# Two-layer cluster attention kernel: the first batch's assignment scores computed as long rows, constants and load holds on another engine, loads in another order

## The chip, the core and the metric

The kernel runs on one core of a Trainium2 chip. The metric is the device time of one execution in microseconds. A core has TensorE (matmuls, results to PSUM), VectorE, ScalarE and GpSimd for elementwise work, and SyncE (SP), whose queue issues the DMAs here. The engines run side by side and wait for each other by semaphores; each works through its own instructions strictly in the order in which the program has them.

## What is computed

Inputs are q, k, v of shape (2, 8, 768, 64): batch, heads, tokens, head size; 16 centroids per head; and four weight matrices. Everything is float32. Each query and each key goes to the centroid with the highest cosine, and a query attends only to keys of its own cluster. Then two MLPs follow.

```python
q_assign = argmax(einsum('bhsd,hcd->bhsc', q_n, c_n), axis=-1)   # same for k
mask = q_assign[:, :, :, None] == k_assign[:, :, None, :]
scores = where(mask, scale * q @ k.T, -1e9)
attn = softmax(scores)                # over keys
x = (attn @ v) -> (1536, 512)
h = x @ w_in;  g = h * clip(h + 3, 0, 6) / 6;  x = g @ w_out      # 512 -> 2048 -> 512
h = x @ w_in2; g = softplus(h);                out = g @ w_out2
```

## The kernel before

**Blocks.** Tokens are worked in six blocks of 256 queries (`b`, `u`: two batches, three blocks each), and in each block eight heads `h` with two chunks `c` of 128 queries: 96 chunks in all. A chunk (`chunk`) is: score matmuls into `s` (L811), the row maximum `nm` on VectorE (L814), the exponential `e` with its sum `sm` on ScalarE (L822), the constants `r0` (L824) and its reciprocal `r` (L826) on VectorE. Block 0 then works in float32: GpSimd makes a diagonal matrix `dg` of `r` (L835), TensorE transposes and scales `e` with it (`tr`, L842), ScalarE or VectorE copies to `pt`, and `avt` multiplies with v (L912). Later blocks split `e` times `r` into two float16 halves `hl` (ScalarE L433, VectorE L441) and transpose by DMA (L850).

**Assignment.** Before a pair of heads `p` can be scored, `assign(b, p)` finds the clusters. For the first batch it takes each 128 tokens of q or k as the stationary operand and streams the 16 centroids of one head past them (L714): 24 float32 matmuls, each of which is two records in the trace. The scores stand token by row in `asc`. VectorE takes the maximum of each 16 (`mx`, L718) and marks it (`eq`, L720); `et` (L725, twelve matmuls into quarters of 32 rows) turns the marks into rows, ScalarE copies them (`eb`, L727), `z` (L729) with the constant matrix `firstb` drops double marks, and VectorE writes the one-hot rows `oh` (L731). `rows` sends these by DMA under q and k (L758 for the first pair, L760 through DRAM for the others), where they carry the mask into the score matmuls. Block 0 has q and k zero-padded from 64 to 128 rows (`load0`).

**Weights.** They come as raw 64-bit words and are decoded on VectorE (`st<-raw`, L499 to L501), scaled by a power of two from a sum over all elements (`ams`, L418) and split into two float16 halves `w`. A raw tile can be written as soon as its buffer is free; to hold its load back, `pace` writes one column of it from the latest `r` on VectorE (L411), and `after` one from an `oh` on GpSimd (L404). The load waits for that write.

**Order.** The program's text, sorted by a table of due times (`plan`, from the numbers `K`), gives the first order. `own_order` then schedules all instructions with estimated durations (`list_schedule`) and fixes each engine's order and each buffer's turn by it. The chip only sees the fixed orders.

Of the kernel before, what the change touches and what calls it, by code (L numbers as in the profile page):

```python
# [24 lines left out]
    'slack': (184, 150),  # L25
    'a0': [-1.034, 0.017, 0.1, 0.301],
    'v0': 0.083,
    'v1': 3.174,
    'a1': [2.227, 2.112, 2.976, 3.115],
    'i': [0.443, 0.618, 0.93, 1.054],  # L30
    'il': [0.3, 0.468, 0.282, 0.282],
    'o': [1.198, 1.398, 1.598, 1.883],
    'ol': [0.192, 0.221, 0.231, 0.162],
    'wd': 0.075,
    'm': [1.41, 2.61, 3.54, 4.619, 5.555],
    'ml': [0.976, 0.75, 1.091, 1.101, 1.097],
# [21 lines left out]
    'w2e': [4.608, 4.84],  # L58
    'w2l': 0.64,
    'w2d': 0.213,  # L60
    't3': 4.134,
    'w2s': 'left',
    'te': [0, 0, 1, 0, 0, 0, 0, 0, 1, 0, 0, 0, 0, 0, 0, 0],
    'dgb': 2,
    'v2': -0.023,
# [5 lines left out]
    'vp': [-0.109, -0.075, -0.065, -0.073],  # L71
    'eqp': [0, 1, 1, 1],
# [30 lines left out]
def estimate(op, eng, ins, outs, inst, psum):  # L103
# [55 lines left out]
def graph(nc):  # L159
# [10 lines left out]
    T, stream = [], []  # L170
# [69 lines left out]
    g.insts, g.E, g.T, g.stream, g.tiles, g.after, g.needs = insts, E, T, stream, tiles, after, needs  # L240
# [4 lines left out]
def list_schedule(g, slack):  # L245
# [49 lines left out]
    for _ in range(N):  # L295
        best = None
        for e, r in ready.items():
            shared = port["Pool" if e == "DVE" else "DVE"] if e in port else 0.0
            for k in r:
                s = max(free[e], at[k])  # L300
                if T[k][2]:
                    s = max(s, shared)
                if best and (s, k) >= best:
                    continue
# [4 lines left out]
                if not best or (s, k) < best:  # L309
                    best = s, k  # L310
# [4 lines left out]
        if e == "PE":  # L315
# [3 lines left out]
            if cold:  # L319
                hold += stream[k]  # L320
# [50 lines left out]
def kernel(ctx: ExitStack, tc: tile.TileContext, qT, kT, v, cen, w1i, w1o, w2i, w2o, out):  # L371
# [208 lines left out]
    cur = {}  # L580
# [47 lines left out]
    cs0 = acon.tile([64, NP, 2, C], F32)  # L628

    def centroids():  # L630
# [70 lines left out]
    def assign(b, p):  # L701
        NT = S // 128
        a = cur["as"].tile([128, 2, NT, 2, C], F32, tag="h", name="asc")
        if b:
            rq, rk = load_q(b, p, slice(0, S), rawq), load_k(b, p)
        for t in range(2):
            for i in range(NT):
                c = slice(i * 128, (i + 1) * 128)
                if b:
                    nc.tensor.matmul(out=a[:, t, i], lhsT=(rq, rk)[t][:, c], rhs=cs[:, p], start=True, stop=True)  # L710
                    continue
# [532 lines left out]
```

## Time and profile before

| | us |
|---|---|
| median of 3 runs | 804.05 |
| lowest to highest | 801.77 to 806.32 |
| the profiled execution | 803.36 |
| its span, first to last instruction | 801.4 |
| TensorE busy | 754.5 (94%) |
| VectorE busy | 496.7 (62%) |
| ScalarE busy | 465.2 (58%) |
| GpSimd busy | 93.0 (12%) |

Busy shares are means over the whole span. The kernel has parts with different limits, so a stretch has to be read by itself. The chain of waits goes back from the last instruction to what released it, and so on to the start: what stands in it was on the path to the end, in that execution.

### The profile page before, as it was taken

How to read it: one execution, taken by the hardware profiler on the slowest of the kernel's cores; microseconds unless marked ns; L12 is line 12 of the kernel's file. 1: busy time of each engine (PE TensorE's matmuls, PEld its weight loads, DVE VectorE, ACT ScalarE, POOL GpSimd, SP SyncE). 2: the span in 40 equal slices, each digit the busy share in tenths (PEclk: the TensorE clock that was granted, in tenths of full speed). 3: DMA queues.
4: the chain of work that ended last, by engine and by line, in shares of the span. 5: the costliest groups of instructions: out<-in, count | busy, mean ns of one | idle time of the engine just before them, and what ended most of it. 6: DMA issues, size and time to landing. Idle time of an engine off the chain costs nothing.

```text
span 801.4 us, 13944 instructions
## 1 busy us (share of the span) xinstructions
PE 754.5 (94%) x5341; PEld 531.1 (66%) x5341; DVE 496.7 (62%) x1016; ACT 465.2 (58%) x797; POOL 93.0 (12%) x77
## 2 busy tenths in 40 slices
PE   5899986789899999989899999999999999999998
PEld 5677664568778888778787888965654444444443
DVE  3256899999987779877889996598342012100200
ACT  1064887777787879856887782668675134321400
POOL 6001720220110120000001000212402000000000
PEclk9998997889999999999999999999999999999999
DMA  8280659788987997889998989145010000000000
GB/s 178 52 281 21 203 186 224 189 189 208 230 219 165 186 193 152 158 176 221 219 183 169 226 198 280 55 141 175 13 40 14 14 13 14 14 13 14 14 27 26
DMA packets 182785, 106.06 MB, mean 132 GB/s; under 512 B 143808, under 2 KB 169280, under 8 KB 182720
## 3 DMA queue, kind: packets, MB, share of 16 engines
q1 hardware_dynamic: 182720, 105.19, 55.6%
q8 instruction: 42, 0.69, 0.4%
q14 instruction: 23, 0.19, 0.1%
HBM read 57.77 MB, written 7.86 MB: 82 GB/s over the span
## 4 chain that ended last, share of the span: by engine, by line
PE 68%; DVE 19%; DMA 7%; issue 3%; ACT 2%; SPq 1%; ACTq 0%; DVEq 0%
PE y L557 9%; PE y L558 9%; PE y L556 9%; PE h L556 8%; PE h L558 8%; PE h L557 8%; PE s L811 6%; PE asc L714 4%; PE avt L916 3%; DVE nm L814 3%; DVE hl L441 3%; DMA pt<-hl 2%; DMA raw<-in_moe_w_in_dram 2%; DVE st L500 2%; DVE w L441 2%
## 5 line engine op out<-in xcount | busy, mean ns | idle before, releaser
L556 PE MATMUL y<-g,w 128*128 128x256 f16 (+1 forms) x576 | 177.6, 309 | 1.3 <-ACT ys L997 1.3
L557 PE MATMUL y<-g,w 128*128 128x256 f16 (+1 forms) x576 | 177.6, 308 | 0.9 <-DVE g L441 0.9
L558 PE MATMUL y<-g,w 128*128 128x256 f16 (+1 forms) x576 | 177.5, 308 | 0.0
L556 PEld LDWEIGHTS <-w 128*128 128x128 f16 x1152 | 114.9, 100 | 62.7 <-issue 8.4
L557 PEld LDWEIGHTS <-w 128*128 128x128 f16 x1152 | 113.7, 99 | 63.1 <-issue 9.2
L558 PEld LDWEIGHTS <-w 128*128 128x128 f16 x1152 | 113.6, 99 | 60.4 <-issue 5.7
L441 DVE SCALAR_TENSOR_TENSOR g<-a,sg,g 128x512 f16<-128x512 f32 x48 | 37.1, 804 | 143.7 <-ACT g L433 143.6
L556 PE MATMUL h<-x,w 128*128 128x256 f16 x384 | 107.1, 279 | 3.2 <-DVE r L980 2.2
L557 PE MATMUL h<-x,w 128*128 128x256 f16 x384 | 106.7, 278 | 0.0
L558 PE MATMUL h<-x,w 128*128 128x256 f16 x384 | 106.7, 278 | 0.0
L822 ACT ACTIVATE e<-s,nm 128x768 f32<-128x768 f32 x96 | 85.7, 893 | 25.2 <-DVE nm L818 8.9
L814 DVE TENSOR_REDUCE nm<-s 128x1 f32<-128x768 f32 x96 | 90.8, 948 | 15.3 <-PE s L811 15.0
L441 DVE SCALAR_TENSOR_TENSOR hl<-e,r,hl 128x768 f16<-128x768 f32 x80 | 80.5, 1011 | 11.7 <-ACT hl L433 11.4
L433 ACT ACTIVATE hl<-e,r 128x768 f16<-128x768 f32 x80 | 73.6, 927 | 15.4 <-DMA pt<-hl 11.0
L557 PE MATMUL h<-y,w 128*128 128x512 f16 x192 | 72.8, 379 | 0.0
L558 PE MATMUL h<-y,w 128*128 128x512 f16 x192 | 72.8, 379 | 0.0
L556 PE MATMUL h<-y,w 128*128 128x512 f16 x192 | 72.6, 379 | 0.0
L1143 ACT ACTIVATE a<-h,c 128x512 f32<-128x512 f32 x48 | 31.9, 682 | 68.7 <-PE h L558 68.7
L916 PE MATMUL avt<-pt,v 128*64 128x256 f16 x720 | 52.3, 288 | 3.8 <-DMA pt<-hl 3.2
L811 PE MATMUL s<-kb,qb 128*128 128x384 f32 x160 | 49.8, 391 | 4.7 <-ACT e L822 3.1
L1181 ACT ACTIVATE os<-y,c 128x512 f32<-128x512 f32 (+1 forms) x13 | 8.4, 654 | 76.8 <-PE y L558 76.8
L787 POOL TENSOR_TENSOR kb<-rk,kb 64x768 fp32r<-64x768 f32 x16 | 31.7, 1984 | 153.0 <-ACT kb L786 152.6
(154 smaller groups left out, 1104.0 us busy)
## 6 DMA issues: line engine op xcount, KB each, us to landing
raw<-in_moe_w_out_dram SPq DMA_DIRECT2D x32, 512.0 KB, 4.8
raw<-in_moe_w_in_dram SPq DMA_DIRECT2D x8, 1024.0 KB, 7.6
raw<-in_moe_w_in_dram SPq DMA_DIRECT2D x16, 512.0 KB, 4.7
ka<-kb SPq DMA_DIRECT2D x40, 192.0 KB, 3.3
qd<-in_q_dram SPq DMA_DIRECT2D x80, 64.0 KB, 3.2
rk<-in_k_dram SPq DMA_DIRECT2D x12, 384.0 KB, 3.9
st<-in_v_dram SPq DMA_DIRECT2D x12, 256.0 KB, 4.1
ydram<-ys SPq DMA_DIRECT2D x12, 256.0 KB, 2.7
```

Source lines behind the costliest of these rows:

```text
L433: nc.scalar.activation(out=hi, in_=src, func=ACTF.Copy, scale=scale)
L441: nc.vector.scalar_tensor_tensor(out=lo, in0=src, scalar=scale, in1=hi, op0=ALU.mult, op1=ALU.subtract)
L556: nc.tensor.matmul(out=ps, lhsT=wt.lhsT(kk, m, 0), rhs=xh, start=start, stop=False)
L557: nc.tensor.matmul(out=ps, lhsT=wt.lhsT(kk, m, 0), rhs=xl, start=False, stop=False)
L558: nc.tensor.matmul(out=ps, lhsT=wt.lhsT(kk, m, 1), rhs=xh, start=False, stop=stop)
L714: nc.tensor.matmul(out=a[:, t, i, odd], lhsT=x[:, c], rhs=cs0[:, p, odd], start=True, stop=True)
L787: nc.gpsimd.tensor_tensor(out=kb[there], in0=rk[here], in1=kb[here].bitcast(F32), op=ALU.subtract)
L811: nc.tensor.matmul(out=s[:, n, 0:SH], lhsT=x[:, q], rhs=y[:, n * SH:(n + 1) * SH], start=i == 0, stop=i == len(pairs) - 1)
L814: nc.vector.tensor_reduce(out=nm, in_=sv, op=ALU.max, axis=AX.XY, negate=True)
L822: nc.scalar.activation(out=e.rearrange("p (a s) -> p a s", a=2), in_=sv, func=ACTF.Exp, bias=nm, scale=scale, accum_out=sm)
L916: nc.tensor.matmul(out=a[64 * odd:64 * odd + 64, p % 2, :], lhsT=vt[:, kt, vi, odd, :], rhs=PT[2 * p + odd][:, pi * KT + kt, :], start=(kt ...
L1143: nc.scalar.activation(out=a, in_=h, func=ACTF.Softplus, scale=cj)
```

## The change

- **Scores as long rows** (`assign`, first batch only). The centroids are now the stationary operand, 32 columns (one head's 16 and 16 zeros), and 384 tokens of q or k stream past them; eight matmuls, two for each quarter of 32 rows of one PSUM tile `asc`. ScalarE copies it to `sa`; three transposes on TensorE give `at`, token by row, for `mx` and `eq`. `et` is now three matmuls of 128 columns. `cs0` gets 128 rows and zeros. For pairs 0 to 2, `at` and `z` lie in another PSUM pool.
- **Constants.** `r0` is computed on GpSimd in blocks 2, 3 and 4 (48 chunks).
- **Holds.** `pace` uses GpSimd's `after` instead of a VectorE copy.
- **Order.** The planner has a limit on how far the DMA queue may run ahead (`back`), expects DMA results 800 ns late instead of 184, prices float32 matmuls otherwise, and the table `K` has new numbers.
- `right` and the pairs in `G` are assertions at build time; they make no instruction.

```diff
 K = {
-    'slack': (184, 150),
+    'slack': (800, 150),
+    'asx': 3,
+    'back': 10000,
+    'pcp': 1,
+    'r0p': [2, 3, 4],
...
@@ list_schedule
+            floor = queue - K["back"] if e == "SP" else 0.0
...
-                s = max(free[e], at[k])
+                s = max(free[e], at[k], floor)
...
@@ pace
         if 0 in paced:
-            nc.vector.tensor_copy(out=tile_[:, 0:1].bitcast(F32), in_=paced[0])
+            if K["pcp"]:
+                after(tile_, paced[0])
+            else:
+                nc.vector.tensor_copy(out=tile_[:, 0:1].bitcast(F32), in_=paced[0])
@@ centroids
-    cs0 = acon.tile([64, NP, 2, C], F32)
+    cs0 = acon.tile([128, NP, 2, 2, C], F32)
...
-        nc.vector.tensor_copy(out=cs0, in_=ctv[0:64])
+        for half in range(2):
+            nc.vector.tensor_copy(out=cs0[0:64, :, half, half, :], in_=ctv[0:64, :, half, :])
@@ assign, first batch
-                for odd in range(2):
-                    x = (Q0[p][0:64, odd], K0[2 * p + odd][0:64])[t]
-                    nc.tensor.matmul(out=a[:, t, i, odd], lhsT=x[:, c], rhs=cs0[:, p, odd], start=True, stop=True)
+            ac = cur["as"].tile([128, SH], F32, tag="h", name="asc")
+            for r in range(4):
+                t, n = divmod(r, 2)
                 for odd in range(2):
+                    x = (Q0[p][:, odd], K0[2 * p + odd])[t][:, n * SH:(n + 1) * SH]
+                    nc.tensor.matmul(out=ac[32 * r:32 * r + 32, :], lhsT=cs0[:, p, odd].rearrange("p a c -> p (a c)"), rhs=x, start=odd == 0, stop=odd == 1)
+            sa = asp.tile([128, SH], F32, tag="sa", name="sa")
+            nc.scalar.activation(out=sa, in_=ac, func=ACTF.Copy)
+            pool, tag = (ps_a, "a") if p < K["asx"] else (cur["as"], "h")
+            a = pool.tile([128, H2, 128], F32, tag=tag, name="at")
+            for i in range(H2):
+                nc.tensor.transpose(out=a[:, i, :], in_=sa[:, i * 128:(i + 1) * 128], identity=ident)
...
+            for i in range(H2):
+                nc.tensor.matmul(out=et[:, i * 128:(i + 1) * 128], lhsT=eq[:, i * 128:(i + 1) * 128], rhs=identb, start=True, stop=True)
@@ chunk
-        nc.vector.tensor_scalar(out=r0, in0=sm, scalar1=1e-9, scalar2=P14, op0=ALU.add, op1=ALU.mult)
+        (nc.gpsimd if (b * NU + u) in K["r0p"] else nc.vector).tensor_scalar(out=r0, in0=sm, scalar1=1e-9, scalar2=P14, op0=ALU.add, op1=ALU.mult)
```

Two places show how the order moves. TensorE, from the end of the first assignment on, before (L714 is an assignment's scores; q_184 and k_187 are the first pair's q and k, q_193 and k_196 the second's):

```order
L729 LDWEIGHTS firstb
L729 MATMUL z<-eb,firstb 128x384
L714 MATMUL asc<-cs_156,q_193 128x16 x12
L714 MATMUL asc<-cs_156,k_196 128x16
L714 MATMUL asc<-cs_156,k_199 128x16
```

And changed, from the second pair's first scores to the first score matmuls of attention (L735 is the new form; q_195, k_198 and k_201 are the second pair's, q_186 and k_189 the first's):

```order
L735 MATMUL asc<-q_195,cs_156 32x384
L760 LDWEIGHTS firstb
L760 MATMUL z<-eb,firstb 128x384
L735 MATMUL asc<-q_195,cs_156 32x384 x3
L735 MATMUL asc<-k_198,cs_156 32x384
L735 MATMUL asc<-k_201,cs_156 32x384
L735 MATMUL asc<-k_198,cs_156 32x384
L735 MATMUL asc<-k_201,cs_156 32x384
L741 MATMUL at<-ident,sa 128x128 x3
L849 MATMUL s<-k_189,q_186 128x384 x2
```

The second pair's scores now begin ahead of the first pair's `z`, and the second pair's transposes stand ahead of the first `s`. On VectorE the operations that build `firstb` stood behind the first `eq`; now all but the last two stand ahead of the first `mx`.

GpSimd, in blocks 0 and 1, before (L404 is a hold on `oh`, L835 `dg`, L787 the `kb` subtraction of the next block's keys):

```order
L404 TENSOR_SCALAR rk<-oh 128x1 x2
L835 TENSOR_SCALAR dg<-ident,r 128x128 x2
L787 TENSOR_TENSOR kb<-rk,kb 64x768
L835 TENSOR_SCALAR dg<-ident,r 128x128
L787 TENSOR_TENSOR kb<-rk,kb 64x768 x2
```

And changed (L416 is a hold, on `oh` or on `r`; L874 `dg`, L818 `kb`):

```order
L416 TENSOR_SCALAR rk<-oh 128x1 x2
L874 TENSOR_SCALAR dg<-ident,r 128x128 x2
L416 TENSOR_SCALAR raw<-r 128x1
L818 TENSOR_TENSOR kb<-rk,kb 64x768
L874 TENSOR_SCALAR dg<-ident,r 128x128
L818 TENSOR_TENSOR kb<-rk,kb 64x768
L874 TENSOR_SCALAR dg<-ident,r 128x128
L416 TENSOR_SCALAR raw<-r 128x1
L416 TENSOR_SCALAR qd<-r 128x1
L416 TENSOR_SCALAR raw<-r 128x1
L874 TENSOR_SCALAR dg<-ident,r 128x128
```

The holds of `raw`, `qd` and `rk` now stand between `dg` and `kb`. On VectorE, 32 `raw` copies, two of `rk` and one of `qd` are gone, and so are 48 of the 96 `r0`. Between VectorE's 17th and 33rd `nm`, where 12 `w<-st,wf` of L441 stood, 8 stand now, and the other four behind; one `hl`, one `mx` and four decode operations have also gone behind it, and two `qb` have come in.

## Rows read from the trace of the kernel before

**Rows 1.** Stretches: us; busy of PE, PEld, DVE, ACT, POOL; clock; DMA share; GB/s.
```profile
33.80:112.20 78.40, 74.81 (x444) 53.91 (x441) 55.19 (x129) 47.00 (x87) 24.75 (x27) 0.93 0.54 169
112.20:205.60 93.40, 74.41 (x564) 59.17 (x563) 92.93 (x196) 73.81 (x131) 10.49 (x6) 0.87 0.87 200
205.60:472.70 267.10, 258.53 (x2344) 216.09 (x2344) 228.50 (x457) 207.14 (x376) 21.02 (x12) 0.98 0.91 190
```

**Rows 2.** Two `nm` reductions in the timeline: start us, us, engine, line.
```profile
112.16 0.94 DVE L814 TENSOR_REDUCE nm<-s 128x1 f32<-128x768 f32 x1
...
205.56 0.93 DVE L814 TENSOR_REDUCE nm<-s 128x1 f32<-128x768 f32 x1
```

**Rows 3.** The chain that ended last, in order of time: start us, us, what.
```profile
6.64 10.43 PE asc L714 x48
...
33.85 1.58 PE s L811 x2
...
35.75 3.84 PE s L811 x6
...
51.92 6.15 PE asc L714 x48
...
58.07 2.86 PE tr L842 x12
...
60.93 2.54 PE s L811 x4
...
65.48 1.45 PE avt L912 x12
...
66.93 1.53 PE tr L842 x12
...
68.47 5.67 PE asc L714 x48
...
77.00 1.34 PE s L811 x4
```

**Rows 4.** Stretches of 2 us: TensorE busy us, granted clock, DMA share, GB/s.
```profile
6.00:8.00 2.00, 1.63 (x8) 1.00 1.01 212
...
36.00:38.00 2.00, 2.00 (x4) 1.00 0.31 96
...
58.00:60.00 2.00, 2.00 (x10) 0.50 0.04 16
```

**Rows 5.** The first assignment's steps in the timeline.
```profile
17.10 0.56 DVE L718 TENSOR_REDUCE mx<-asc 128x24 f32<-128x384 f32 x1 [10.14 <-PE asc L714]
...
18.92 0.49 ACT L727 ACTIVATE eb<-et 128x384 bf16<-128x384 f32 x1 [15.66 <-PE et L725]
...
20.39 0.50 PE L729 MATMUL z<-eb,firstb 128*128 128x384 bf16 x1 [1.55 <-DVE firstb L624]
...
20.92 0.68 DVE L731 TENSOR_SCALAR oh<-z,lim 128x384 f32<-128x384 f32 x1 [0.60 <-PE z L729]
...
22.95 1.22 SPq L758 DMA_DIRECT2D q<-oh  x2
```

**Rows 6.** The landing of its rows (DMA issues: KB each, us to landing).
```profile
q<-oh SPq DMA_DIRECT2D x4, 24.0 KB, 2.4
```

**Rows 7.** TensorE in the timeline where two tile shapes follow each other.
```profile
63.40 0.37 PE L725 MATMUL et<-identb,eq 128*32 128x128 bf16 x12
63.71 1.51 PE L912 MATMUL avt<-pt,st 128*64 128x256 f32 x10
```

**Rows 8.** VectorE from 112 to 206 us, groups: busy us, mean ns, idle before.
```profile
L441 DVE SCALAR_TENSOR_TENSOR w<-st,wf,w 128x512 f16<-128x512 f32 x12 | 10.0, 868 | 0.0
...
L411 DVE COPY raw<-r 128x1 f32<-128x1 f32 x15 | 1.8, 142 | 0.0
```

**Rows 9.** GpSimd's `dg`: the group of 16, then one in the timeline.
```profile
L835 POOL TENSOR_SCALAR dg<-ident,r 128x128 f32<-128x128 f32 x16 | 15.6, 977 | 43.2 <-DVE r L826 16.0 <-PE tr L842 7.0 <-DVE st L499 6.5
...
68.62 1.96 POOL L835 TENSOR_SCALAR dg<-ident,r 128x128 f32<-128x128 f32 x1 [6.52 <-DVE st L499]
```

More of the change, by code (lines that the diff above doesn't have):

```diff
@@ L57 @@
     'ze': [0],
[L58 to L61, printed above, removed]
+    'w2e': [4.647, 4.705],
+    'w2l': 0.276,
+    'w2d': 0.437,
+    't3': 4.102,
     'w2s': 'left',
[L63 removed]
+    'te': [1, 0, 1, 0, 0, 0, 0, 0, 1, 0, 1, 0, 0, 0, 0, 0],
     'dgb': 2,
[L65 removed]
+    'v2': -0.269,
     'dge': 0,
@@ L169, in graph @@
     wrote, read, bank = {}, {}, {}
-    T, stream = [], []
+    T, stream, cold = [], [], []
     def cells(a):
@@ L192, in graph @@
         stream.append(elements(ins[0]) * min(i.tile_size[1], 128) / 76.8 if E[k] == "PE" and str(ins[0].dtype) == "dt.float32" else elements(ins[0]) / 2.4 if E[k] == "PE" else 0.0)
+        cold.append(max(stream[k], 1.75 * i.tile_size[1]) if E[k] == "PE" and str(ins[0].dtype) == "dt.float32" else stream[k])
         T.append(estimate(i.opcode, E[k], ins, outs, i, psum))
@@ L239, in graph @@
     g = Graph()
-    g.insts, g.E, g.T, g.stream, g.tiles, g.after, g.needs = insts, E, T, stream, tiles, after, needs
+    g.insts, g.E, g.T, g.stream, g.cold, g.tiles, g.after, g.needs = insts, E, T, stream, cold, tiles, after, needs
     g.users, g.group, g.order, g.bufs, g.pool = users, group, order, bufs, pool
@@ L308, in list_schedule @@
                 s = max(s, w)
-                if not best or (s, k) < best:
-                    best = s, k
+                least = min(least, s)
+                own.append((k, s))
+            own = [(s, k) for k, s in sorted(own) if s <= least + look][:1]
+            if own and (best is None or own[0] < best):
+                best = own[0]
         s, k = best
@@ L319, in list_schedule @@
             if cold:
-                hold += stream[k]
+                hold += g.cold[k]
                 done = hold + 170
@@ L721, in assign @@
         et = cur["as"].tile([128, SH], F32, tag="h", name="et")
-        for t in range(2):
-            for i in range(NT):
-                r0, c0 = 32 * (2 * t + i * 128 // SH), i * 128 % SH
-                nc.tensor.matmul(out=et[r0:r0 + 32, c0:c0 + 128], lhsT=eq[:, (t * NT + i) * 32:(t * NT + i + 1) * 32], rhs=identb, start=True, stop=True)
+        if b:
+            for t in range(2):
+                for i in range(NT):
+                    r0, c0 = 32 * (2 * t + i // H2), i % H2 * 128
+                    nc.tensor.matmul(out=et[r0:r0 + 32, c0:c0 + 128], lhsT=eq[:, (i * 2 + t) * 32:(i * 2 + t + 1) * 32], rhs=identb, start=True, stop=True)
+        else:
+            for i in range(H2):
+                nc.tensor.matmul(out=et[:, i * 128:(i + 1) * 128], lhsT=eq[:, i * 128:(i + 1) * 128], rhs=identb, start=True, stop=True)
         eb = asp.tile([128, SH], BF16, tag="eb", name="eb")
         nc.scalar.activation(out=eb, in_=et, func=ACTF.Copy)
-        z = cur["as"].tile([128, SH], F32, tag="h", name="z")
+        pool, tag = (ps_a, "a") if b == 0 and p < K["asx"] else (cur["as"], "h")
+        z = pool.tile([128, SH], F32, tag=tag, name="z")
         nc.tensor.matmul(out=z, lhsT=firstb, rhs=eb, start=True, stop=True)
@@ L798, in prep, with right @@
         KQ[h] = (qa, qb, ka, kb)
+        of["q", h] = b, u
         rows(b, u, h)
     PT = {}
+    of = {}
+    def right(which, b, u, h):
+        if of.get((which, h), (0, 0)) != (b, u):
+            raise ValueError("another block's tile")
     def chunk(b, u, h, c):
         p, odd = divmod(h, 2)
+        right("q", b, u, h)
         qa, qb, ka, kb = KQ[h] if b + u else (Q0[p][:, odd], None, K0[h], None)
@@ L990, in l2 @@
             for kk in range(4 * part, 4 * part + 4):
-                g = G[kk // 2]
+                of, g = G[kk // 2]
+                if of != i:
+                    raise ValueError("a later block's g")
                 mm3(y[:, m % 2, :], W1O, kk, m, g[:, 0, kk % 2, :], g[:, 1, kk % 2, :], kk == 0, kk == KF - 1)
```

66 lines of the change are left out of this document (36 added, 30 removed).

## Prediction

> **What bounds the kernel now.** I read the busy time of long stretches first, then the chain of waits, then single rows where the chain passes the code that changes. In the stretches [rows 1] one engine after another is full. From 33.8 to 112.2 us TensorE is busy 74.8 of 78.4 us. From 112.2 to 205.6, VectorE is busy 92.9 of 93.4 us and TensorE only 74.4. From 205.6 on TensorE is nearly full again (258.5 of 267.1 us), and so it stays to the end. The borders are no accident: at 112.16 and 205.56 the 17th and the 33rd of the 96 `nm` reductions start [rows 2], one for each chunk, so the first stretch is block 0's sixteen chunks and the second is block 1's. Before 33.8 us there are only the first two assignments.
>
> The chain of waits [rows 3] shows what the first stretches consist of. The assignment's `asc` matmuls hold 10.43 us of it from 6.64, the same again from 21.66 for the second pair of heads, 6.15 us from 51.92 and 5.67 us from 68.47: 32.7 us, all on TensorE and all on the path. The first score matmul, `s`, starts only at 33.85. Two things are to be seen in the single times. First, an `asc` record costs the same however little it streams: 16 columns, but 10.43/48 = 0.22 us. Second, TensorE runs at two speeds. `s` takes 3.84/6 = 0.64 us at 35.75 and 1.34/4 = 0.335 us at 77.00; twelve `tr` take 2.86 us at 58.07 and 1.53 us at 66.93. The granted clock [rows 4] prints 0.50, that is 1.2 GHz, in 58 to 60 (and so again in 74 to 76), each time just after one of the two later `asc` runs; around 36 us it prints 1.00, but the 0.64 us of `s` says that TensorE was at the lower level there too, as it was under the first two `asc` runs (0.22 us a record, against 5.67/48 = 0.12 at 68.47).
>
> **The change part by part.** *Scores as long rows.* Of the first batch's four assignments each had 24 float32 matmuls (48 records), which go. In come 8 matmuls of 384 columns into 32 output rows (16 records), a ScalarE copy `sa`, and three transposes (6 records). No row of before shows a float32 matmul into 32 columns. The nearest is the first block's `avt`, 64 columns wide, with neighbours that alternate between the two halves of the array: 12 records of 256 columns in 1.45 us [rows 3], 0.121 us each; scaled to 384 columns 0.181. Lower bound: all four quarters run at once, four records deep, by `s` 4 x 0.335 = 1.34 us at full clock and 2.56 us at the lower one. Upper bound: none overlap, 16 x 0.335 = 5.4 us or 10.2 us. I take the `avt` price, since two neighbours in a row go to one quarter here: 2.9 us at full clock, 5.8 us at the lower one. The transposes are priced by `tr`: 6/12 of 1.53 = 0.77 us, or of 2.86 = 1.43 us.
>
> *Start.* Assignment 0 begins at 6.64 as before, since the same centroid chain releases it. Scores to 12.4; `sa`, priced as the copy `eb`, 0.49 us and a hand-over of 0.1 [rows 5], to 13.0; transposes to 14.4. From `mx` (17.10) to the end of `oh` (20.92 + 0.68 = 21.60) the trace has 4.50 us [rows 5], in which `z` at 20.39 waited 1.55 us for `firstb`. The order now builds `firstb`'s parts ahead of `mx`, so `z` can start 0.1 us behind `eb` (18.92 + 0.49), at 19.5, not 20.4: 0.9 us less; two short VectorE operations get in between, by the price of a hold 0.2 us each with their gaps [rows 8]. So 4.0 us, and `oh` ends at 18.4 instead of 21.6. Its rows then go out by four DMA issues, of which the last begins 0.6 us before 24.17 and lands 2.4 us later [rows 5, 6]: 4.4 us after `oh`, 22.8. Meanwhile TensorE does the second assignment: one matmul ahead of `z`, seven behind it (14 x 0.36 at the lower clock = 5.1 us, to about 22.6), `sa` 0.6, transposes 1.4. The order puts the first `s` behind these, so it starts at 24.6 instead of 33.85: **9.2 us**. With the lower bound it is 13: the scores end at 10.5, since k's second half is the sixth load (1.6 MB at 212 GB/s [rows 4] from 2.4 us on lands at 10), `oh` at 16.4, and the rows land at 20.8. With the upper bound it is 0.7: scores to 16.9, `z` at 22, then 14 x 0.64 and 2 us more, so `s` at 33.1.
>
> *Assignments 2 and 3* lie inside the stretch where TensorE is full. They had 6.15 + 5.67 = 11.8 us and will have 2 x (2.9 + 0.77) = 7.3: **4.5 us** (bounds 7.6 and -0.5). *Clock:* what ran at 1.2 GHz behind those two `asc` runs was twelve `tr` (2.86 against 1.53) and `s` (2.54 against 1.34) at 58.07 to 63.5, and a second such `tr` run at 74: 1.3 + 1.2 + 1.3 = **3.8 us**. The new records stream 384 columns as `s` does, and behind runs of `s` and `avt` the clock doesn't fall in these stretches; I take all of it, with 0 as the other end.
>
> A rule speaks against this part. The trace has 12 `et` of 32 columns at 63.40 and `avt`, with another shape, at 63.71 [rows 7]: no idle stands between them. The Trainium skill (TensorEngine Tiling, Key Properties) says that changing the tiling mode drains TensorE; the trace gives no visible price for it. The same section says that different tiles run in parallel, which is the lower bound above, and one of the rivals.
>
> *Constants and holds to GpSimd.* Between the 17th and the 33rd `nm`, VectorE now has 15 `raw` holds at 0.142 us [rows 8], which go (2.1 us). The order also moves work out of this stretch to behind it: four `w<-st,wf` at 0.868 us [rows 8] (3.5 us), and one `hl`, one `mx` and four decode operations, while two `qb` move in; I put these six at half of that row each, 2.6 us. VectorE is full there, so up to 8.2 us. But DMA is at 0.87 of its time in that stretch [rows 1]; in 85 us it would be at 0.96. I take half, 4.1, and take back 2 us, since the order also leaves TensorE that much more to do behind the 33rd chunk: **2.1 us**. Constants `r0` of blocks 2 to 4 (48 operations) leave VectorE where it is busy 228.5 of 267.1 us while TensorE is full [rows 1]: nothing, and what hides it is TensorE. If that cover went, each would cost what a `dg` takes more than a hold, 0.84 us [rows 8, 9].
>
> *Loads.* The order of SP's queue moves v's loads behind the first weight loads, and little else. The queue's bounded backlog changes what the planner believes; with DMA at 0.54 in the first stretch I cost it at nothing, with 4 us either way for the 8.6 us that TensorE still waits in 205.6 to 472.7 [rows 1].
>
> Sum: 9.2 + 4.5 + 3.8 + 2.1 = 19.6 us. The profiled execution took 803.36 us for its span of 801.4, so 783.8 us; the median of the runs is 0.7 us above it. I say **784 us**.
>
> **The rivals.** *Four quarters at once*: 13 + 7.6 + 3.8, and with it the whole 8.2 us of VectorE's stretch, 32.6: 771 us. For it: the 12 `et` of 32 columns issue within 0.31 us [rows 7], 26 ns each. Against it: two matmuls in a row go to one quarter. (This is the Trainium skill's rule on tiles, named above.)
>
> *No overlap*: the new form doesn't shorten what it replaces: 0.7 - 0.5 + 3.8 + 2.1 = 6.1, so 797 us. Against it: `avt` at 0.121 us, where one stream of 256 columns by the `s` row would be 0.22.
>
> *GpSimd's holds in the way.* A hold stands in front of a load, in GpSimd's strict order, between `dg` and `kb`; the SP queue and VectorE's decode wait behind it. GpSimd operations next to VectorE's are slow at times: `dg`, 128 columns, takes 0.977 us on average and 1.96 us at 68.62 [rows 9]. If each of the 15 holds delays its load by that mean, all of it on the path, 15 x (0.98 - 0.14) = 12.6 us of the gain is lost: 796 us. At 1.96 us each it is 27.3 us, and the kernel is **slower, 811 us**. The point from which it is slower is 19.6/15 + 0.14 = 1.4 us a hold. Against it: GpSimd is busy 10.5 of 93.4 us in that stretch [rows 1], and a load sent a microsecond late mostly lands in time. For it, the Trainium skill (GPSIMD Engine Reference, Specifications) says that GpSimd shares its SBUF interfaces with VectorE; the two times of `dg` don't speak against it, and no row here shows the cause.
>
> **How the numbers follow.** Forecast 784 (777 to 791 on its own): 0.50. Four quarters, 771: 0.20. No overlap, 797: 0.13. Holds at 1 us, 796: 0.10. Holds at 2 us, 811: 0.07. A measurement of this kernel tells about 0.5% from no change, 4 us. Faster by more than that: 0.5 + 0.2 and most of the two at 796 and 797, 0.88. Within it 0.06, slower 0.06. The range leaves out the slow case and the far end of the quick one: 769 to 798 us, which holds about 0.85.
>
> **What would show it.** The first `s` at 24 to 25 us (21 under four quarters, 33 without overlap), 16 `asc` records in about 5.8 us at the start and 2.9 us later; a granted clock that doesn't fall to 0.50 behind assignments 2 and 3; the 17th `nm` at about 95 us instead of 112.2, and the 33rd at about 184 instead of 205.6; from there to the end 595 to 600 us as now (801.4 - 205.6 = 596). The forecast is wrong if the gain at the 17th `nm` is gone at the 33rd, or if TensorE idles more than 9 us between the 33rd and the 96th. Holds in the way would show as SP's loads waiting for GpSimd, and VectorE idle before a decode.

## The result, and the profile after

The changed kernel takes **784.7 us** (median of 4 runs, 782.4 to 786.5) beside 804.1 us for the kernel before: a ratio of 0.976, 95% interval 0.972 to 0.980. The forecast was 784.0 us in a range of 769 to 798. The profiled execution took 783.7 us for a span of 781.7.

The stretches of [rows 1], cut at the same events (the first `s`, the 17th, 33rd and 96th `nm`), read after the change (us; busy of PE, PEld, DVE, ACT, POOL; clock; DMA share; GB/s):

```profile
23.40:89.40 66.00, 61.56 (x373) 40.17 (x374) 55.28 (x124) 46.57 (x87) 23.34 (x37) 1.00 0.64 199
89.40:178.20 88.80, 68.53 (x502) 53.04 (x502) 86.98 (x163) 68.63 (x121) 17.84 (x23) 0.83 0.85 197
178.20:447.20 269.00, 258.37 (x2394) 218.42 (x2392) 217.40 (x392) 205.88 (x377) 28.67 (x65) 1.00 0.94 187
447.20:781.70 334.50, 324.85 (x1880) 180.55 (x1880) 124.16 (x226) 140.79 (x209) 36.06 (x16) 1.00 0.21 65
```

The two `nm` that answer to [rows 2], in the timeline:

```profile
89.43 0.96 DVE L852 TENSOR_REDUCE nm<-s 128x1 f32<-128x768 f32 x1 [0.19 <-PE s L849]
...
178.20 0.94 DVE L852 TENSOR_REDUCE nm<-s 128x1 f32<-128x768 f32 x1
```

The 33rd `nm` is 27.4 us earlier than it was, but the end only 19.7 us: the changed kernel gives 7.7 us back behind it. To see why, I split each stretch's length into TensorE's idle time, the time it lost to the lower clock, and the rest. The loss is worked out from stretches of 2 us: busy time times (1 - granted clock), summed. It is the time that the same work would have saved at a clock of 1.00. Where VectorE is full, as in block 1, it need not lengthen the stretch.

| stretch | before | after | work at full clock | clock loss | TensorE idle |
|---|---|---|---|---|---|
| to the first `s` | 33.8 | 23.4 | | | |
| block 0 (to the 17th `nm`) | 78.4 | 66.0 | 69.7 to 61.6 | 5.1 to 0.0 | 3.6 to 4.4 |
| block 1 (to the 33rd) | 93.4 | 88.8 | 65.2 to 57.8 | 9.2 to 10.7 | 19.0 to 20.3 |
| 33rd to 96th | 267.1 | 269.0 | 253.7 to 258.4 | 4.8 to 0.0 | 8.6 to 10.6 |
| behind the 96th | 328.7 | 334.5 | 323.9 to 324.8 | 0.0 to 0.0 | 4.8 to 9.7 |

Three readings follow. Block 0 lost 8.1 us of work and 5.1 us of low clock. Block 1 lost 7.4 us of TensorE work, of which 4.7 stand behind the 33rd `nm` now: 50 more records there (2394 against 2344), 34 of `y` and 18 of the second batch's `asc` among them, by the groups of the two stretches. That they lengthen the stretch by only 1.9 us is due to the clock, which fell twice there before and no longer does. And behind the 96th `nm` TensorE idles 4.9 us longer. Its waits there:

```profile
PE h L572 <- DVE y L456: 1.7, 1, 1.7
PE h L571 <- DVE p2u L439: 1.6, 1, 1.6
PE y L572 <- DVE g L456: 1.6, 1, 1.6
PE ams L433 <- ACT w L518: 0.8, 1, 0.8
```

(Who waited for whom: us in total, times, longest.) Before, one wait for `g` (0.9 us) was all that stood there. VectorE has 124.2 us of work in this stretch instead of 110.5: weights of the second MLP that are decoded later, 26 `st<-raw` steps of each kind where there were 22. One of these groups:

```profile
L516 DVE SCALAR_TENSOR_TENSOR st<-raw,st 128x512 int32<-128x512 int32 x26 | 19.2, 757 | 0.0
```

The chain of waits shows the new start, in answer to [rows 3] (start us, us, what):

```profile
3.93 7.36 DMA k<-in_k_dram
11.28 0.14 issue
11.42 2.79 PE asc L735 x6
14.23 0.50 ACT sa L737
14.77 0.56 PE at L741 x3
15.36 0.56 DVE mx L744
...
17.61 1.46 PE asc L735 x2
19.07 0.45 PE z L760
19.54 0.69 DVE oh L762
...
21.51 1.86 DMA q<-oh
23.41 1.56 PE s L849 x4
...
25.14 0.70 PE s L849 x2
...
26.10 0.65 PE s L849 x2
26.75 1.45 PE asc L735 x16
28.19 0.84 PE s L849 x2
29.04 1.41 PE tr L881 x12
```

An assignment's scores are the line at 26.75: 16 records in 1.45 us, where [rows 3] had 48 in 6.15. The twelve `tr` behind it take 1.41 us, the price of the full clock, not the 2.86 us that they took behind `asc` before. In the timeline the records of q and of k run side by side, first of the third assignment, then of the second:

```profile
26.68 0.52 PE L735 MATMUL asc<-q,cs 128*32 128x384 f32 x2
26.70 0.52 PE L735 MATMUL asc<-k,cs 128*32 128x384 f32 x2
```

```profile
19.45 0.86 PE L735 MATMUL asc<-k,cs 128*32 128x384 f32 x2
...
21.19 0.49 PE L735 MATMUL asc<-q,cs 128*32 128x384 f32 x1
```

The second assignment's correct what stands at the top, that an engine works through its instructions strictly in the order of the program. In the order of the second pair all of q's matmuls stand ahead of k's; in the trace k's first records start at 19.45 and q's last one at 21.19. Records for one quarter of the rows started here while earlier instructions for another were still to start.

In answer to [rows 4], stretches of 2 us (columns as above) at the start and behind the third and fourth assignments:

```profile
18.00:20.00 2.00, 2.00 (x7) 0.32 (x9) 0.46 (x1) 0.00 (x0) 0.00 (x0) 0.50 0.50 95
20.00:22.00 2.00, 1.69 (x14) 0.41 (x6) 0.21 (x1) 0.13 (x1) 0.00 (x0) 0.75 0.05 12
22.00:24.00 2.00, 1.13 (x5) 0.76 (x6) 0.97 (x2) 0.36 (x1) 0.00 (x0) 1.00 0.16 37
28.00:30.00 2.00, 2.00 (x16) 1.47 (x13) 0.73 (x5) 1.37 (x3) 0.39 (x2) 1.00 0.29 99
52.00:54.00 2.00, 2.00 (x22) 1.27 (x14) 1.39 (x4) 2.00 (x5) 0.68 (x1) 1.00 0.82 218
```

GpSimd's operations, in answer to [rows 9] (busy, mean ns, idle before):

```profile
L874 POOL TENSOR_SCALAR dg<-ident,r 128x128 f32<-128x128 f32 x16 | 12.6, 788 | 40.2 <-DVE r L864 18.1 <-DVE nm L856 11.1 <-PE z L760 5.5
...
L416 POOL TENSOR_SCALAR raw<-r 128x1 f32<-128x1 f32 x32 | 9.7, 309 | 116.8 <-DVE r L864 62.9 <-DVE r L862 17.0 <-issue 14.5
```

A hold of `raw` takes 0.31 us on average, and GpSimd's share of the chain of waits is 0%.

### The profile page after: what moved, and what is told of

The parts are those of the page before. It is cut to its first block, busy times and chain, and to the rows that moved or that the text cites. A ratio compares the mean times of both kernels' runs of the same rounds, so it can differ in the third digit from the quotient of the medians.

```text
span 781.7 us, 13710 instructions
## 1 busy us (share of the span) xinstructions
PE 724.9 (93%) x5189; PEld 495.6 (63%) x5189; DVE 491.5 (63%) x936; ACT 465.4 (60%) x799; POOL 118.2 (15%) x161
## 4 chain that ended last, share of the span: by engine, by line
PE 58%; DVE 17%; DMA 9%; ACT 7%; issue 5%; SPq 3%; ACTq 0%; POOL 0%; DVEq 0%
PE h L571 8%; PE h L573 8%; PE h L572 8%; PE y L571 7%; PE y L573 7%; PE y L572 7%; PE s L849 5%; DMA pt<-hl 5%; PE avt L957 4%; DVE st L515 2%; DVE st L516 2%; DVE nm L852 2%; DVE hl L456 2%; PE tr L881 2%; DMA raw<-in_moe_w_out_dram 2%
## 5 line engine op out<-in xcount | busy, mean ns | idle before, releaser
L571 PEld LDWEIGHTS <-w 128*128 128x128 f16 x1152 | 115.6, 100 | 68.2 <-issue 10.9
L456 DVE SCALAR_TENSOR_TENSOR g<-a,sg,g 128x512 f16<-128x512 f32 x48 | 38.7, 836 | 127.6 <-ACT g L448 127.5
L571 PE MATMUL h<-x,w 128*128 128x256 f16 x384 | 109.0, 284 | 7.0 <-DVE r L1021 4.2
L573 PE MATMUL h<-x,w 128*128 128x256 f16 x384 | 108.7, 283 | 0.0
L572 PE MATMUL h<-x,w 128*128 128x256 f16 x384 | 108.6, 283 | 0.0
L957 PE MATMUL avt<-pt,v 128*64 128x256 f16 x720 | 49.0, 275 | 4.7 <-DMA pt<-hl 4.5
L957 PEld LDWEIGHTS <-v 128*64 128x64 f16 x720 | 39.6, 110 | 10.9 <-issue 8.2
```

Of the source, the lines that this page charges most:

```text
L456: nc.vector.scalar_tensor_tensor(out=lo, in0=src, scalar=scale, in1=hi, op0=ALU.mult, op1=ALU.subtract)
L571: nc.tensor.matmul(out=ps, lhsT=wt.lhsT(kk, m, 0), rhs=xh, start=start, stop=False)
L572: nc.tensor.matmul(out=ps, lhsT=wt.lhsT(kk, m, 0), rhs=xl, start=False, stop=False)
L573: nc.tensor.matmul(out=ps, lhsT=wt.lhsT(kk, m, 1), rhs=xh, start=False, stop=stop)
L957: nc.tensor.matmul(out=a[64 * odd:64 * odd + 64, p % 2, :], lhsT=vt[:, kt, vi, odd, :], rhs=PT[2 * p + odd][:, pi * KT + kt, :], start=(kt ...
```

## The experiments

Each kernel's instructions are ordered anew by the planner, so an edit changes more than its own lines. That turned out to matter, and the last four kernels test it. The stage lengths of all of them, in us, with the clock loss in brackets, from one profiled execution each:

| kernel | median | to first `s` | block 0 | block 1 | 33rd to 96th | behind |
|---|---|---|---|---|---|---|
| before | 804.1 | 33.8 | 78.4 (5.1) | 93.4 (9.2) | 267.1 (4.8) | 328.7 |
| after | 784.7 | 23.4 | 66.0 (0) | 88.8 (10.7) | 269.0 (0) | 334.5 |
| e1 full width | 808.3 | 28.3 | 82.2 (3.4) | 87.0 (7.0) | 270.8 (0) | 332.4 |
| e2 old scores | 814.9 | 30.5 | 84.8 (6.8) | 92.5 (8.3) | 271.4 (6.7) | 333.5 |
| e3 scores only | 793.5 | 22.4 | 72.8 (2.9) | 91.4 (10.9) | 271.2 (1.7) | 330.9 |
| e4 old W2 numbers | 786.5 | 23.2 | 67.3 (0) | 89.0 (11.1) | 280.7 (6.8) | 328.1 |
| e5 holds on VectorE | 792.4 | 22.9 | 73.0 (3.4) | 90.1 (11.6) | 273.6 (6.5) | 334.1 |
| e6 constants on VectorE | 788.6 | 23.7 | 67.1 (0) | 89.0 (11.0) | 271.5 (3.4) | 334.2 |
| e7 old load rules | 793.9 | 22.0 | 72.4 (0) | 86.9 (9.4) | 276.6 (8.3) | 332.7 |
| e8 one load later | 786.4 | 22.0 | 68.0 (1.7) | 95.3 (7.9) | 264.8 (2.9) | 334.2 |
| e9 numbers of before | 792.4 | 22.8 | 70.9 (1.7) | 98.0 (8.0) | 269.4 (6.2) | 331.2 |
| e10 lag nudged | 785.9 | 23.5 | 66.7 (0) | 89.0 (11.6) | 272.1 (4.7) | 333.3 |
| e11 step nudged | 792.9 | 23.1 | 68.8 (0) | 88.9 (8.4) | 277.8 (7.6) | 333.5 |
| e12 old tail numbers | 784.4 | 22.9 | 66.0 (0) | 89.0 (11.1) | 269.3 (1.7) | 334.2 |

**e1, full width.** The eight matmuls of an assignment fill all 128 output rows; their stationary operand is zero outside of the quarter that they are for, so no two can run in different quarters. The centroids are copied into that operand, `strip`, before each half; TensorE waits 0.26 us for the second copy.

```diff
-    nc.tensor.matmul(out=ac[32 * r:32 * r + 32, :], lhsT=cs0[:, p, odd].rearrange("p a c -> p (a c)"), rhs=x, start=odd == 0, stop=odd == 1)
...
+    nc.vector.tensor_copy(out=strip[0:64, 112:128], in_=cs0[:, p, odd, :])
...
+    w0 = 112 - 16 * odd - 32 * r
+    nc.tensor.matmul(out=ac, lhsT=strip[:, w0:w0 + 128], rhs=x, start=r + odd == 0, stop=r + odd == 4)
```

> The changed kernel, but the stationary operand of the first batch's scores is padded with zeros to 128 columns, so that all eight matmuls of an assignment write all 128 rows and none can run beside another. The sum of products is the same. Theory (the gain of the long rows comes from four quarters running at once): 16 asc records take 16 x 0.335 = 5.4 us at full clock instead of the 1.45 us seen, 10 us at the lower one; the first assignment ends near 17 instead of 14.2 us, the first s comes at 29 to 31 instead of 23.4 us, assignments 2 and 3 cost 4 us more each, 796 to 800 us in all against 784.7. Rival (the gain is in streaming tokens instead of loading them as weights, and overlap is worth little, since DMA and VectorE set the pace at the start anyway): within 3 us of the changed kernel, 783 to 788.

808.3 us (802.5 to 811.6), ratio to before 1.006 (1.003 to 1.008). The timeline has the price of a record without the overlap:

```profile
39.31 1.45 PE L738 MATMUL asc<-q,strip 128*128 128x384 f32 x4
40.60 1.45 PE L738 MATMUL asc<-k,strip 128*128 128x384 f32 x4
41.89 1.45 PE L852 MATMUL s<-k,q 128*128 128x384 f32 x4
```

From 39.31 to the next `s` at 41.89 eight records take 2.58 us, so sixteen would take 5.2, against 1.45 us in the changed kernel. Twice 3.7 us in block 0 and 4.9 us at the start are 12.3 of the 19.0 us between the two spans. The rest is 6.2 us more idle time and 3.4 us of low clock in block 0, less some 2 us by which the later stretches are shorter. The profiled execution is the quickest of ten; the medians lie 23.6 us apart. So without the four quarters at once the whole change was no gain. That the rest beyond the 12.3 us is the overlap's too is not shown: the copies and the new order are in it.

**e2, old scores.** The changed kernel with `asc` and `et` as they were before.

```diff
-    nc.tensor.matmul(out=ac[32 * r:32 * r + 32, :], lhsT=cs0[:, p, odd].rearrange("p a c -> p (a c)"), rhs=x, start=odd == 0, stop=odd == 1)
...
-    nc.scalar.activation(out=sa, in_=ac, func=ACTF.Copy)
...
-    nc.tensor.transpose(out=a[:, i, :], in_=sa[:, i * 128:(i + 1) * 128], identity=ident)
...
+    nc.tensor.matmul(out=a[:, t, i, odd], lhsT=x[:, c], rhs=cs0[0:64, p, odd, odd], start=True, stop=True)
```

> The changed kernel with the first batch's scores in the old form (tokens as stationary operand, 16 columns streamed), everything else of the change kept, planner and numbers too. Theory (the scores are the front's gain): first s near 33 us again instead of 23.4, 17th nm at 105 to 112 instead of 89.4, 803 to 807 us; the granted clock falls to 0.50 behind assignments 2 and 3. Rival (the front is faster by the order and the numbers): 785 to 793 us.

814.9 us, ratio 1.012 (1.009 to 1.015): **slower than before**, by more than either side expected. Every other part of the change and its numbers, without the scores, cost 10 us. The clock falls again in block 0 (6.8 us lost).

**e3, scores only.** The kernel before, with the new scores, the pool of `at` and `z` included; numbers and planner stay. Against the kernel before:

```diff
-    nc.tensor.matmul(out=a[:, t, i, odd], lhsT=x[:, c], rhs=cs0[:, p, odd], start=True, stop=True)
+    nc.tensor.matmul(out=ac[32 * r:32 * r + 32, :], lhsT=cs0[:, p, odd].rearrange("p a c -> p (a c)"), rhs=x, start=odd == 0, stop=odd == 1)
...
+    nc.scalar.activation(out=sa, in_=ac, func=ACTF.Copy)
...
+    nc.tensor.transpose(out=a[:, i, :], in_=sa[:, i * 128:(i + 1) * 128], identity=ident)
```

> The kernel before with the long-row scores alone; constants, holds, load order and all numbers as before. Theory (the scores are the whole gain, and what the rest gives up to the 33rd nm it loses behind the 96th): first s at 23 to 25 us, 17th nm near 90, stretch from the 96th nm to the end 329 as before and not 334.5; 779 to 784 us. Rival (holds on GpSimd and the new numbers are needed to carry the front's gain through the second block): 17th nm near 90, but 33rd nm at 190 or later, 790 to 797 us.

793.5 us, ratio 0.986 (0.982 to 0.989), as the rival had it. The start is as early as after (22.4), but block 0 gains only 5.6 us: TensorE idles 9.3 us there (before 3.6, after 4.4) and still loses 2.9 us to the clock. Scores alone are worth 11 us; the rest alone costs 10; together they are worth 20. The parts don't add up, so they meet somewhere; e9 to e11 ask whether in the order.

**e4, old W2 numbers.** The numbers that place the second MLP's weights are those of before.

```diff
-    'w2o': [1, 7, 9, 13], 'ly': 6, 'w2': [0.07, 0.411, 0.555, 0.809], 'w2e': [4.647, 4.705], 'w2l': 0.276, 'w2d': 0.437, 't3': 4.102,
+    'w2o': [2, 8, 10, 16], 'ly': 0, 'w2': [-0.049, 0.292, 0.436, 0.7], 'w2e': [4.608, 4.84], 'w2l': 0.64, 'w2d': 0.213, 't3': 4.134,
```

> The changed kernel with the numbers that place the second MLP's weights (w2e, w2l, w2d, t3, w2o, w2, ly) as before. Theory (the 5.8 us that the changed kernel loses behind the 96th nm come from decoding these weights later): stretch from the 96th nm to the end 329 to 331 us instead of 334.5, TensorE idle there 1 to 2 us instead of 7, 779 to 782 us. Rival (the loss is there because attention ends earlier and the rest has not become shorter): 334 us again, 783 to 787.

786.5 us, ratio 0.977 (0.973 to 0.982). The last stretch falls by 6.4 us, as the theory said (3.5 us less idle time, 2.9 us of work that moved ahead of the 96th `nm`), but the one ahead of it grows by 11.7 in the profiled execution. That was the slowest of four runs (790.2 us; the quickest had 783.1, at a mean clock of 0.981 instead of 0.971). Of the 11.7, 6.8 are low clock and 3.5 are work. So the tail's loss comes from these numbers, yet undoing them gave no time back in all. The theory's total fell; so did the rival's tail of 334 us.

**e5 to e8, one part undone each.** In e5 the holds are back on VectorE, in e6 the constants, in e7 the two rules on loads are those of before, and in e8 one load of the second batch's q held until the centroids are there, so that the first k half that TensorE waits for (3.93 to 11.28 in the chain) comes earlier. The four edits, in this order:

```diff
-    'pcp': 1,
+    'pcp': 0,
```

```diff
-    'r0p': [2, 3, 4],
+    'r0p': [],
```

```diff
-    'slack': (800, 150),
+    'slack': (184, 150),
...
-    'back': 10000,
+    'back': 1e9,
```

```diff
+        if b == 1 and p == 1:
+            after(rq, cs.rearrange("p n a c -> p (n a c)"))
```

> The changed kernel with the holds of loads back on VectorE (a copy of one column), the rest of the change kept. Theory (a hold costs VectorE 0.14 us and GpSimd nothing that matters): between the 17th and the 33rd nm, where VectorE is full, 15 holds cost 2 us, 786 to 788 us against 784.7. Rival (holds in GpSimd's strict order delay loads, behind the 33rd nm above all, where TensorE now idles 7 us more than before): 777 to 783 us, and the stretch from the 33rd nm to the end nearer 596 than 603.

> The changed kernel with the constants r0 of all blocks back on VectorE. Theory (VectorE has slack where TensorE is full): no change, 783 to 787 us, 33rd to 96th nm 269 us. Rival a (the hop ScalarE to GpSimd to VectorE lengthens each chunk's chain and makes the transposes late for avt): 779 to 782, less waiting of avt for pt. Rival b (VectorE is full often enough behind the 33rd nm): 788 to 792, 33rd to 96th nm 273 us or more.

> The changed kernel planned with the old expectation of DMA results (184 ns late instead of 800) and without the limit on the queue's backlog; numbers and code as in the change. Theory (no term of the sum rests on it): within 4 us of 784.7, first s at 23.4 us. Rival (the rule carries part of the front's gain, since loads would again stand in front of what is needed first): 17th nm at 94 us or later, 789 to 796 us.

> The changed kernel, but the second batch's first q load (393 KB, fifth in the queue) is held until the centroids are ready, so that the k load that the first assignment waits for (7.36 us in the chain of waits, landing at 11.4) stands ahead of it. Theory (DMA sets the first assignment's end): k lands near 9.5, first s near 21.5 instead of 23.4, and the 17th nm 2 us earlier; 782 to 784 us. Rival (given back, because the second assignment or VectorE sets the pace): first s at 23 or the 17th nm at 89 to 90 all the same, 784 to 786 us.

Measured: e5 792.4 (ratio 0.985, 0.981 to 0.988), e6 788.6 (0.979, 0.976 to 0.982), e7 793.9 (0.986, 0.983 to 0.989), e8 786.4 (0.977, 0.971 to 0.982). By these the holds would be worth 8 us, the constants 4, the rules 9; the prediction had none of them so high. e5 lies outside of both of its ranges; e6 and e7 lie in a rival's, and e7 with the late 17th `nm` that its rival named (22.0 + 72.4 = 94.4), though its first `s` came early. But the table shows another thing: in the profiled executions of e5, e6 and e7 the stretch from the 33rd to the 96th `nm` lost 3.4 to 8.3 us to the clock, where the changed kernel lost none. Only e6's edit is about this stretch alone (blocks 2 to 4). e8's first `s` did come 1.4 us earlier, but the 17th `nm` at 90.0, as its rival had it, and block 1 became 6.5 us longer. So I asked how much the order alone does.

**e9, numbers of before.** The work is the changed kernel's; every number of the plan's table that had changed is back, but for those that switch the other parts (some of them here). One of them says on which engine a copy runs, so two of block 0's sixteen `pt` copies go from VectorE to ScalarE; all else is order.

```diff
-    'v0': 0.208, 'v1': 3.208, 'wd': 0.089, 'lag0': -0.029, 'lag': 0.247, 'v2': -0.269, 'eqp': [0, 1, 1, 0],
+    'v0': 0.083, 'v1': 3.174, 'wd': 0.075, 'lag0': 0.009, 'lag': 0.039, 'v2': -0.023, 'eqp': [0, 1, 1, 1],
```

> The changed kernel with every number of the plan's table that the change altered put back to the value of before (when loads, decodes, recombinations and attention steps are due); the new scores, GpSimd's holds and constants and the two load rules stay. The work is the same to the instruction, only its order moves. Theory: the work itself, not the retuned numbers, carries the gain ahead of the 33rd nm: 782 to 790 us, with the 33rd nm by 185. Rival: the single undos cost so much (786 to 815 us) because each plan is set by all the numbers together, and the numbers of before fit the new work no better than the undone kernels did: 791 to 803 us, lost in the stretches between the first s and the 33rd nm.

792.4 us, ratio 0.986 (0.983 to 0.989), the rival's side: 12 us of the gain need no new numbers, some 8 us do. They are lost in blocks 0 and 1 (4.9 and 9.2 us), and part of that comes back in the tail. Beside e3 it says more. Both have the new scores and the numbers of before; e9 has GpSimd's holds and constants, the load rules and the planner's new prices in addition, and takes 792.4 us where e3 takes 793.5 (0.986 both). With those numbers the other parts together are worth about 1 us, within the noise; the 4 to 9 us of e5 to e7 appear only with the numbers that were tuned to the whole. New numbers on the scores alone were not tried.

**e10 and e11, one number nudged.** No work is changed.

```diff
-    'lag': 0.247,
+    'lag': 0.24,
```

```diff
-    'wd': 0.089,
+    'wd': 0.085,
```

> The changed kernel with one number of the plan moved by 3 per cent: the due time of every attention step but a unit's first 0.247 to 0.240. Nothing is added, removed or replaced; about 550 rows on VectorE and many on TensorE stand elsewhere. It asks how far the order alone moves the time. Theory: a nudge moves the time by at most 2 us (782 to 787), so that the undos of 4 us and more (constants, holds, load rules) are prices of the parts undone. Rival: a nudge alone costs 3 to 10 us (788 to 795), and the prices of the undos below that are not told apart from the order.

> The changed kernel with another number of the plan moved by 4 per cent: the time between a weight group's decode steps 0.089 to 0.085. Same question as the lag. Theory: 782 to 787 us. Rival: 788 to 795 us.

e10: 785.9 us, ratio 0.978 (0.976 to 0.981), the theory. e11: **792.9 us**, 0.986 (0.983 to 0.989), the rival. A number moved by 4 per cent costs 8 us, as much as undoing the holds or the load rules. Between the 33rd and the 96th `nm` e11 is 8.8 us longer than the changed kernel, and 7.6 us of that are clock. Stretches of 4 us of e11:

```profile
196.00:200.00 4.00, 3.86 (x28) 3.48 (x27) 4.00 (x7) 3.22 (x5) 3.23 (x4) 0.93 1.12 216
200.00:204.00 4.00, 2.26 (x27) 1.44 (x28) 3.33 (x4) 1.64 (x3) 1.62 (x2) 0.50 0.91 257
204.00:208.00 4.00, 4.00 (x27) 2.24 (x27) 3.36 (x6) 1.51 (x3) 0.00 (x0) 0.50 0.78 220
208.00:212.00 4.00, 3.81 (x15) 3.20 (x15) 3.06 (x9) 3.06 (x8) 0.00 (x0) 0.50 1.03 249
```

and of the changed kernel:

```profile
188.00:192.00 4.00, 2.95 (x33) 2.10 (x31) 3.94 (x9) 3.52 (x8) 0.85 (x3) 1.00 1.09 345
192.00:196.00 4.00, 4.00 (x37) 3.60 (x34) 3.91 (x8) 3.48 (x6) 2.18 (x2) 1.00 0.93 224
196.00:200.00 4.00, 4.00 (x55) 3.03 (x55) 3.12 (x6) 2.84 (x6) 2.02 (x2) 1.00 1.14 194
200.00:204.00 4.00, 3.47 (x27) 2.77 (x26) 3.97 (x10) 3.63 (x8) 0.48 (x1) 1.00 1.07 349
```

What stands at this place is an assignment of the second batch, whose scores still have the old form: 24 records that stream 32 columns each. In the timeline of the changed kernel, of e11 and of e4 (start us, us):

```profile
192.70 1.42 PE L727 MATMUL asc<-cs,rq 128*128 128x32 f32 x12
193.96 1.50 PE L727 MATMUL asc<-cs,rk 128*128 128x32 f32 x12
```

```profile
197.17 1.52 PE L727 MATMUL asc<-cs,rq 128*128 128x32 f32 x12
198.53 1.94 PE L727 MATMUL asc<-cs,rk 128*128 128x32 f32 x12
```

```profile
195.41 2.60 PE L727 MATMUL asc<-cs,rq 128*128 128x32 f32 x12
197.82 2.75 PE L727 MATMUL asc<-cs,rk 128*128 128x32 f32 x12
```

The changed kernel gets through this run at full clock (1.50 us for twelve). In e11 the clock falls within it, and in e4 it has fallen about 2 us ahead of it, behind a stretch of 4 us in which TensorE was busy 2.67 us; there twelve take 2.75. Stretches of e4:

```profile
188.00:192.00 4.00, 2.67 (x25) 2.15 (x22) 3.97 (x9) 2.29 (x5) 0.83 (x3) 1.00 1.03 290
192.00:196.00 4.00, 3.90 (x30) 2.93 (x30) 3.96 (x7) 3.40 (x7) 1.60 (x2) 0.68 1.20 242
```

In both kernels the clock stays at 0.50 for about 14 us, and what stands behind the run pays for it. Both had idle time on TensorE shortly before the fall (e11 3.53 of 4 us busy at 192), but so had the changed kernel (2.95 of 4 us busy at 188), without a fall; what tips it these runs don't settle.

Nor do they show that the order fixes the falls, or that these are the 8 us. Each run has its mean clock on record: the changed kernel's four lie between 0.967 and 0.978, and the one at 0.967 took 786.5 us, while e11 took 792.2 at 0.974, e5 791.6 at 0.976 and e7 794.7 at 0.976. The clock accounts for most of the difference between the two profiled executions in this stretch; what makes up the difference of the medians stays open.

**e12, old tail numbers.** Of e4's edit, only these:

```diff
-    'w2o': [1, 7, 9, 13], 'ly': 6, 'w2': [0.07, 0.411, 0.555, 0.809],
+    'w2o': [2, 8, 10, 16], 'ly': 0, 'w2': [-0.049, 0.292, 0.436, 0.7],
```

> The changed kernel with only the numbers that place the second MLP's weights behind the 96th nm put back (w2o, ly and w2); those that place its first decodes ahead of it (w2e, w2l, w2d, t3) stay as changed. Undoing both moved 6 us from the tail into the stretch before it. Theory: the tail's loss hangs on its own numbers: the tail falls from 334.5 to 329-331 with 33rd to 96th nm at 269, 778 to 781 us. Rival: the tail is long because two column groups of weights are still to be decoded there, whatever their due times: tail 333 to 336, 783 to 787 us.

784.4 us, ratio 0.978 (0.973 to 0.983), tail 334.2: the rival. By elimination, the tail hangs on the other numbers of e4 (`w2e`, `w2l`, `w2d`, `t3`), which place the first decodes ahead of the 96th `nm`, or on both sets together. No kernel of these beats the changed one by more than the measurement tells.

## Why the prediction was right, and what in it was not

The total was right to 1 us, and start, scores and clock moved as forecast. The fourth term, 4.1 less 2, came out at 4.6 less 7.7. That the total was so close is luck: the scores were priced too dear by 3.3 us, the tail was left out with 5.8, and smaller misses made up the rest.

**Start: forecast 9.2 us, measured 10.4.** The first `s` came at 23.41, forecast 24.6. On the way two steps missed. The scores ended at 14.2 instead of 12.4, since TensorE waited for k until 11.28; the lower bound had that load in it (10), the forecast did not. And `z` no longer waits for `firstb`, as said, but for two `asc` records of the second pair at 17.61, which take 1.46 us at the lower clock; the text named one matmul ahead of `z` and charged nothing for it. So `oh` ended at 20.2, forecast 18.4. What made it good was the second assignment: its 14 records were charged 5.1 us at the lower clock, and from 19.43 they were through by 21.7. So the last wait was another than forecast: not TensorE's own work but the landing of q's rows at 23.37.

**Assignments 2 and 3: forecast 4.5 us, measured 7.8.** This is the term that was mis-sized. I priced a record by `avt` at 0.181 us (2.9 us an assignment); the chain has 1.45 us for 16, 0.091 us each, a hair above the lower bound of 1.34. The reason given against the bound, that two neighbours in a row go to one quarter, did not count: records for other quarters run meanwhile, as the timeline rows of q and k show. With `at` at 0.56 us an assignment takes 2.0 us, and 11.8 - 2 x 2.0 = 7.8. The bound for *four quarters at once* said 7.6. e1 shows the other end: 5.2 us for 16. As to the rule that changing the tiling mode drains TensorE (the Trainium skill, TensorEngine Tiling (Array Packing), Key Properties): no run here shows a price; all 16 records together took 0.11 us over the bound. In the changed kernel's chain the 32-column run at 26.75 follows on an `s` that ends at 26.75, and the next `s` starts at 28.19.

**Clock: forecast 3.8 us, measured about 4.1.** Block 0's loss went from 5.1 us to none, and there is no fall behind the third and fourth assignments. But the clock fell before the old `asc` runs ended, at 58.07 and 74.14, as two stretches of before show:

```profile
56.00:58.00 2.00, 2.00 (x13) 1.97 (x12) 0.00 (x0) 0.00 (x0) 0.00 (x0) 0.63 0.72 281
...
72.00:74.00 2.00, 2.00 (x18) 2.00 (x17) 0.00 (x0) 0.00 (x0) 0.00 (x0) 0.89 0.00 0
```

So 1.0 of the 5.1 us is in the 11.8 us of the scores already. A gain of the same kind was in no term: the first eight `s` took 1.58 + 3.84 us before (the last six 0.64 us each, under a printed clock of 1.00 [rows 3, 4]), and take 1.56 + 0.70 + 0.65 now, 2.5 us less. The printed clock doesn't show it, so it stands under work in the table.

**Block 1: forecast 4.1 us, measured 4.6.** VectorE's busy time there fell by 5.9 us, and the stretch by 4.6.

**Behind the 33rd `nm`: forecast 2 us given back, measured 7.7.** The term missing from the sum is the tail, 5.8 us. The working charged nothing for the retuned numbers that place the second MLP's weights, and expected the rest of the program at 595 to 600 us. It is 603.5: work moved out of block 1 (4.7 us at full clock), hidden by 4.8 us of clock that I had not expected to come back there, 2.0 us more idle, and the later decodes behind the 96th. My own sign for being wrong, TensorE idle for more than 9 us between the 33rd and the 96th `nm`, did appear (10.6 us), and it cost 2 us, not the gain. That the 2 us charged here and the 1.9 us measured in that stretch agree is chance.

So with the right sizes the sum up to the 33rd `nm` is 10.4 + 7.8 + 4.1 + 4.6 = 26.9 us, and 29.4 with the first `s`; 27.4 are measured, with 0.8 us more idle time in block 0 and work that the order moved into it (168 `tr` records against 162). The 7.7 us behind it bring the 27.4 to 19.7. *Four quarters at once* was the truth of the mechanism, and its 771 us was wrong by the give-back, by 3.6 us of VectorE's stretch and by 2.6 us of the start. *Holds in the way* is out: 0.31 us a hold, where 1.4 was its turning point, no step of GpSimd in the chain, and no gain from taking the holds back (e5). Between the 17th and the 33rd `nm` SP waited 3.2 us for GpSimd's holds of `raw`, where it had waited 10.6 us for VectorE's, and no wait of VectorE there is over 0.5 us.

**Loads, constants: forecast nothing.** The undos give 9 and 4 us (e7, e6), the holds' 8 (e5). After e9 and e11 these can't be read as prices of the parts. What may be the parts' own is block 0 in e5 and e7, 7.0 and 6.4 us longer, with 3 to 4 us more idle time on TensorE; whether holds and load rules are worth that by themselves stays open, since e9 lost 4.9 us there with both of them in place.

What is shown, then: the new scores are necessary (e2), and in them the overlap of quarters (e1); the scores by themselves are worth 11 us (e3); and about 8 us of the 20 come with the retuned numbers (e9), that is with the order but for two copies. One nudge of the order takes the same amount away (e11). By what the order makes these 8 us is not shown.

## What to carry to other kernels

Where a small stationary operand leaves most of TensorE's columns empty, stream long rows past it and spread the matmuls over the four quarters of the output rows: 16 float32 records of 384 columns took 1.45 us instead of 5.2. Where a planner orders the program anew after each edit, nudge a number that should not matter before you read an undo as the price of a part: here that alone moved the time by 1 to 8 us. And split a stretch into work, idle time and clock loss before you explain it: in e11 a fall of the clock within a run of short records that took 3.3 us lasted about 14 us. But one profiled execution shows that execution; look at the clocks of the other runs before you put a median down to it.

## What the hardware showed that was not expected

- The four quarters run at once even where two matmuls in a row go to the same quarter: 0.091 us a record, against 0.32 us at full width (e1). Records started out of the program's order for it (k at 19.45, the last of q at 21.19).
- The same run of 24 records of 32 columns was passed at 1.00 in the changed kernel and stood within about 14 us at 0.50, in whole or in part, in e4 and e11. Of the second batch's runs no kernel here has another form; long rows there too were not tried.
- A `[128 x 1]` operation on GpSimd took 0.19 us in most cases, but up to 1.23 us for a hold of `raw` in block 1 and 3.49 us for one of `rk`; nothing on the path waited for them.
